# A whole new order of an attention and softplus-MLP kernel: warm-up tile moved, two batches read by split products, fillers ahead of the scores

## The chip, the cores and the metric

One core of one Trainium2 chip. The metric is the device time of one execution in microseconds, lower is better; 0.3% of it is 2.0 us. Engines: TensorE (PE; its weight loads PEld), VectorE (DVE), ScalarE (ACT), GpSimd (POOL), and SyncE (SP), which here issues every DMA.

## The reference, cut to what matters

```python
# x: (8, 8, 512, 64) = B, H, S, D;  state: (8, 8, 32, 64)
scale = 1.0 / np.sqrt(D)
a  = softmax(scale * x @ state.T)      # (B, H, 512, 32)
xread = a @ state                      # (B, H, 512, 64)
a2 = softmax(scale * state @ x.T)      # (B, H, 32, 512)
sread = a2 @ x                         # (B, H, 32, 64)
rows = concat([xread, sread], axis=2)  # heads side by side: (8 * 544, 512)
h = rows @ w_in                        # 512 -> 2048
out = softplus(h) @ w_out              # 2048 -> 512
```

(softmax subtracts the row's maximum and adds 1e-9 to the sum; softplus is max(h, 0) + log1p(exp(-|h|)). The weights come in as float64.)

## The kernel before, in words

**Work.** A batch's scores `sc` (step Q) serve both softmaxes. The one over the 32 states is done on a tile transposed in blocks: A (transpose), M (maximum), Ms (subtract it), m (exp), N (sum and reciprocal), Nm (multiply), D (transpose back), then the split ah, al. The one over the 512 rows: E (row maximum), e (exp with the sum), r (reciprocal). The states are multiplied into w_in (the V tiles), so that the MLP's hidden layer of a batch's 512 x-rows is one product per block of 128 of the 2048 hidden columns: step `h.b.f`, six matmuls of 512 columns. It is followed by softplus (`s`), its split (`gh`, `gl`) and the second layer `m.b.f.c`, three matmuls each for four row blocks c. The 256 sread rows of all batches go through the MLP together as group 8 (`h.8.u.i`, `m.8.u.i`).

**Splits.** Most products run in TensorE's fast float32r format. An operand is split into a high part (a cast on ScalarE, line 289) and a low part (a subtraction on VectorE, line 305), and three products, high by high, high by low, low by high, are added. The scores Q of batches 0 and 1 and the products V0, V1 of w_in with the states are plain f32 matmuls, which the profile shows as two records each.

**Weights.** w_in and w_out arrive as 64-bit words: `Li`, `Lo` load them, `ch`, `cu`, `cr` convert them (cr joins both halves), `wh`, `wl` split w_out, `Sw` stores converted w_in, `V0`, `V1` multiply w_in by the states, `va`, `ve` copy the products out of PSUM, `vh`, `vl` split them.

**Read of the sread rows.** `Lx` loads x; G transposes the exponentials on TensorE (four 128-column transposes), R multiplies them by x, X scales by 1/sum, T transposes to `sreadT`, which h.8 needs. For batches 2 to 7 the operands of R are split (`ph`, `pl` for the exponentials, `yh`, `yl` for x; R is eight float32r matmuls; `xc`, `xa` add two halves). For batches 0 and 1 (`WHOLE = 2`) `ga` copies the exponentials and R is four plain f32 matmuls.

**Order.** Nothing is reordered at run time. `PLAN` is one list of 2638 steps, `name:engine:places`, in the order in which they are issued; each engine takes its own in that order. Engine letters: T TensorE, V and W VectorE (W another form of `cu` with two instructions), A and C ScalarE (C a form of `ch` by a plain copy), G GpSimd, S SyncE. The number is the slot of SBUF or bank of PSUM; a step that takes a slot waits until every earlier user of that slot is done. Here the list begins

```
Lz.0:S:0 Lt.0.1.0:S:1 Lt.0.1.1:S:2 zn.0:G:3 Li.0.1:S:4 Li.0.0:S:5 Lq.1:S:6 Lq.0:S:7 Li.0.6:S:8 ...
```

and ahead of it the kernel puts the warm-up tile `idle` into slot 0, sets it to zero (line 766) and runs eight f32 matmuls on it (line 768). `Lz.0` then takes slot 0 too. TensorE's first steps are Q.0.1, V1.0.0, V0.0.0, V1.0.1, V0.0.6, Q.0.0, ...; ahead of its first h (`h.0.0`) stand four Q, thirteen V, G.0.1, G.0.0 and R.0.1.

The matmul helper is line 308, DMA loads and stores are lines 296 and 299, copies 289 (ScalarE) and 293 (VectorE), cu 337, 340 and 341, cr 345, A 453, Ms 456, Nm 466.

Of the kernel before, what the change touches and what calls it, by code (L numbers as in the profile page):

```python
# [8 lines left out]
F32 = mybir.dt.float32  # L9
# [28 lines left out]
ch.0.3:A:31 Lo.0:S:2 V0.0.1:T:6 E.0.0:V: va.0.1.1:A: va.0.1.0:A: cu.0.3:V:32 e.0.0:A:33 cr.0.2:V: cr.0.3:V: V0.0.2:T:7 ch.0.7:C:34 A.0.0:V:35
V0.0.3:T:1 e.0.1:A:36 va.0.2.0:V: M.0.0:V: va.0.3.0:A: ch.0.4:A:37 cu.0.4:V:38 vh.0.0:A:39 Lt.1.1.1:S:40 Ms.0.0:V: G.0.1:T:2 va.0.6.1:A: Lx.0.1:S:3
V1.0.6:T:3 va.0.2.1:A: cr.0.4:V: Sw.0.3:S: ch.0.5:A:41 vl.0.0:V:42 V0.0.4:T:6 m.0.0:A: Lt.1.0.1:S:43 ve.0.6:V:44 Lo.1:S:4 va.0.4.0:A: cu.0.5:V:45  # L40
zc.1.0:A: cu.0.7:W:46 Sv.0.6:S: G.0.0:T:5 zc.1.1:A: ga.0.1:A:47 cr.0.5:V: Lo.2:S:5 cr.0.7:V: ch.o0:A:48 Sw.0.4:S: V0.0.5:T:0 cu.o0:V:49 Lo.3:S:6
# [36 lines left out]
Sp.1.2.6:S: vl.0.4:V:6 Lo.14:S:13 P.1.3.7:T:4 Rl.3.1:V: F.1.5.3:S: h.0.8:T:0 Sp.0.3.0:S: vh.1.4:A:40 F.1.5.0:S: Lx.2.1:S:11 wl.9:V:38 pe.1.3.7:A:29
m.0.6.2:T: Sw.3.0:S: s.0.8:A:41 Sp.1.3.7:S: h.0.9:T:4 vl.0.5:V:2 wl.11:V:25 pe.1.2.3:V:18 h.0.11:T:0 ch.3.2:A:4 vl.1.4:V:30 Sp.1.2.3:S: gh.0.8:A:6
# [163 lines left out]
class Op:  # L243
# [594 lines left out]
```

## Time and profile before

| | |
|---|---|
| runs | 678.28, 676.57, 676.0; median 676.57 us |
| profiled execution | 675.82 us, span 674.0 us |
| TensorE busy | 660.8 us (98% of the span), 3028 matmul records |
| VectorE, ScalarE busy | 408.1 and 420.9 us |
| GpSimd busy | 1.6 us |
| DMA | 85.54 MB |

The span runs from the first to the last instruction of the profiled execution; the time has a little more around it. A row of a group gives busy time, the mean of one instruction in ns, and the idle time of the engine just before, with what ended it. Matmuls overlap, so the distance from start to start is what one costs in a stream, not its duration.

### The profile page before, as it was taken

Reading aid. Unit: us, or ns where it says so; the run is one execution under the profiler, and the core shown is the slowest. Engines: PE = TensorE matmul, PEld = TensorE weight load, DVE = VectorE, ACT = ScalarE, POOL = GpSimd, SP = SyncE. Lnnn points to the kernel's source line nnn. Section 1 sums busy time; section 2 is a strip of 40 time slices with the busy share of each in tenths; the row PEclk is TensorE's granted clock in tenths of the full one; section 3 lists DMA queues with packets and bytes.
Section 4 is the critical chain, followed back from the end, with each engine's and each line's share of the span. In section 5 each row is a group of like instructions: output and inputs, shape, how many; then the busy total and the mean of one; then the engine's idle time right before and its main releaser. Section 6 shows DMA issues by size and latency. Waiting matters only on the chain.

```text
span 674.0 us, 8950 instructions
## 1 busy us (share of the span) xinstructions
PE 660.8 (98%) x3028; PEld 540.2 (80%) x3028; DVE 408.1 (61%) x790; ACT 420.9 (62%) x746; POOL 1.6 (0%) x8
## 2 busy tenths in 40 slices
PE   6899999999999999999999999999999999999997
PEld 3576778888888888888888888888888888988886
DVE  3899969786987597452855367445846586122210
ACT  2989986767767787753765367535865658224322
POOL 0000000000000000000000000000000000000000
PEclk9999999999999999999999999999999999999999
DMA  5994368857138324621233122412076202103001
GB/s 206 376 396 154 116 232 275 312 195 236 55 112 248 89 90 134 200 65 51 92 108 88 32 94 79 118 32 94 17 245 177 71 17 79 48 1 78 1 0 63
DMA packets 54094, 85.54 MB, mean 127 GB/s; under 512 B 7456, under 2 KB 28960, under 8 KB 54048
## 3 DMA queue, kind: packets, MB, share of 16 engines
q1 hardware_dynamic: 54048, 84.96, 38.7%
q8 instruction: 24, 0.39, 0.2%
q14 instruction: 22, 0.18, 0.1%
HBM read 57.15 MB, written 27.79 MB: 126 GB/s over the span
## 4 chain that ended last, share of the span: by engine, by line
PE 91%; DVE 4%; DMA 2%; ACT 2%; issue 1%; SPq 0%; ACTq 0%
PE acc L308 53%; PE h L308 28%; PE pp L308 3%; PE rp L308 3%; PE qp L308 2%; PE gp L494 1%; DMA vd<-ve 1%; DMA w<-in_w_in_dram 1%; PE vp L308 1%; DVE wf L345 1%; PE h_idle L768 1%; DVE gL L305 1%; PE sc L308 1%; ACT Vk L289 0%; DVE Vl L305 0%
## 5 line engine op out<-in xcount | busy, mean ns | idle before, releaser
L308 PE MATMUL acc<-Wh,gH 128*128 128x512 f32 x544 | 215.3, 396 | 0.0
L308 PE MATMUL acc<-Wh,gL 128*128 128x512 f32 x544 | 212.1, 390 | 0.1
L308 PE MATMUL acc<-Wl,gH 128*128 128x512 f32 x544 | 212.1, 390 | 0.0
L305 DVE TENSOR_TENSOR gL<-t,gH 128x512 fp32r<-128x512 f32 x136 | 92.3, 686 | 172.5 <-ACT gH L289 172.2
L637 ACT ACTIVATE t<-h 128x512 f32<-128x512 f32 x136 | 79.9, 598 | 168.6 <-PE h L308 168.0
L308 PEld LDWEIGHTS acc<-Wh,gL 128*128 128x128 f32 x544 | 102.1, 188 | 22.8 <-DVE gL L305 1.2
L308 PEld LDWEIGHTS acc<-Wl,gH 128*128 128x128 f32 x544 | 102.2, 188 | 21.2 <-issue 0.9
L308 PEld LDWEIGHTS acc<-Wh,gH 128*128 128x128 f32 x544 | 102.2, 188 | 21.1 <-issue 0.7
L308 PE MATMUL h<-aH,Vh 128*128 128x512 f32 x256 | 101.9, 398 | 0.2 <-ACT Vh L289 0.2
L308 PE MATMUL h<-aH,Vl 128*128 128x512 f32 x256 | 99.9, 390 | 0.1
L308 PE MATMUL h<-aL,Vh 128*128 128x512 f32 x256 | 99.8, 390 | 0.1
L289 ACT CAST gH<-t 128x512 fp32r<-128x512 f32 x136 | 83.3, 623 | 3.5 <-PE acc L308 1.2
L308 PEld LDWEIGHTS h<-aH,Vh 128*128 128x128 f32 x256 | 48.0, 188 | 11.8 <-ACT t L637 0.8
L308 PEld LDWEIGHTS h<-aL,Vh 128*128 128x128 f32 x256 | 48.1, 188 | 10.8 <-DVE aL L305 0.9
L308 PEld LDWEIGHTS h<-aH,Vl 128*128 128x128 f32 x256 | 48.1, 188 | 10.6 <-DVE Vl L305 0.5
L305 DVE TENSOR_TENSOR Vl<-Vf,Vh 128x512 fp32r<-128x512 f32 x56 | 37.9, 683 | 10.4 <-ACT Vh L289 5.5
L289 ACT CAST Vh<-Vf 128x512 fp32r<-128x512 f32 x56 | 34.5, 620 | 2.2 <-DMA Vf<-vd 2.1
L289 ACT COPY o<-acc 128x512 f32<-128x512 f32 x30 | 16.9, 590 | 12.8 <-PE acc L308 12.4
L637 ACT ACT_TABLE_LOAD x18 | 23.1, 1283 | 2.8 <-issue 2.1
L308 PE MATMUL h<-sreadT,uH 128*128 128x256 f32 x128 | 23.4, 283 | 0.0
L308 PEld LDWEIGHTS h<-sreadT,uH 128*128 128x128 f32 x128 | 20.6, 191 | 0.8
L577 DVE TENSOR_TENSOR sc<-qp,qs 64x512 f32<-64x512 f32 x24 | 16.4, 683 | 8.0 <-ACT qs L575 7.5
(113 smaller groups left out, 726.9 us busy)
## 6 DMA issues: line engine op xcount, KB each, us to landing
vd<-px SPq DMA_DIRECT2D x48, 256.0 KB, 3.8
Vf<-vd SPq DMA_DIRECT2D x192, 64.0 KB, 2.0
xT<-in_xt_dram SPq DMA_DIRECT2D x32, 256.0 KB, 4.7
o<-in_w_out_dram SPq DMA_DIRECT2D x16, 512.0 KB, 6.7
x<-in_xn_dram SPq DMA_DIRECT2D x16, 512.0 KB, 4.7
out_dram<-o SPq DMA_DIRECT2D x32, 256.0 KB, 2.1
w<-in_w_in_dram SPq DMA_DIRECT2D x12, 512.0 KB, 6.5
Wf<-wsc SPq DMA_DIRECT2D x32, 128.0 KB, 2.8
```

The costliest lines, as they stand in the source:

```text
L289: nc.scalar.copy(dst, src)
L305: lambda e: eng(e).tensor_tensor(r(dlo()), src(), dhi(), ALU.subtract))
L308: nc.tensor.matmul(dst, lhs, rhs, start=start, stop=stop)
L345: nc.vector.scalar_tensor_tensor(u, page(f"h2.{key}", n).bitcast(I32), 3, u, ALU.logical_shift_left, ALU.bitwise_or)
L494: nc.tensor.transpose(at(f"gp.{b}.{g}")[:, P * c:P * c + P], at(src)[:, P * c:P * c + P], at("ident"))
L577: lambda e, kj=kj, sc=sc, j=j: nc.vector.tensor_tensor(at(sc)[64 * j:64 * j + 64], at(f"qp.{kj}")[0:64], at(f"qs.{kj}")[0:64], ALU.add))
L637: lambda e: nc.scalar.activation(at(f"t.{k}"), at(f"h.{k}"), AF.Softplus))
L768: nc.tensor.matmul(at("h.idle")[:, 0:P], at("idle")[:, 0:P], at("idle")[:, 0:P], start=True, stop=True)
```

## The change

- `PLAN` is written anew: order, engines and places of all steps (2636 steps). TensorE's last 382 steps are in the old order.
- The warm-up tile gets a place of its own; the first load is into a fresh slot.
- xT of a batch is one load of 1 MB in a slot of four pages (kind `q`) instead of four loads of 256 KB; batch 0's is the first load of all.
- Batches 0 and 1 read as the others do: the code of batches 2 to 7 moves into `readrows` and serves all; `ga` and the f32 R go, and T turns two 64-column blocks instead of four of 128.
- 13 elementwise steps of the head go to GpSimd: Ms and Nm of batches 0 and 1, vh.0.0, al.0.1, ah.1.0, ah.1.1, al.1.0.
- Fillers `w.i`, two transposes of the identity, may stand in the plan; six do, all ahead of the first h.
- The partial outputs of batches 0 and 1 lie in one tile `po` each instead of four.
- Six `pe` copies more run on ScalarE instead of VectorE, and two more `cu` in the W form.

TensorE's first steps now: Q.0.0, V1.0.1, Q.0.1, V0.0.3, five fillers, V1.0.0, V0.0.1, V1.0.3, V1.0.7, a filler, V0.0.7, V0.0.0, V0.0.2, V1.0.2, Q.1.1, Q.1.0, V0.0.4, V0.0.5, V0.0.6, h.0.1, h.0.0, ... The G and R steps of batch 0 come later.

```diff
+WARMERS = 60
 PLAN = """
-Lz.0:S:0 Lt.0.1.0:S:1 Lt.0.1.1:S:2 zn.0:G:3 Li.0.1:S:4 Li.0.0:S:5 Lq.1:S:6 Lq.0:S:7 Li.0.6:S:8 Lt.0.0.0:S:9 zc.0.0:V: zc.0.1:V: Lt.0.0.1:S:10
...
+Lt.0:S:0 Lz.0:S:1 zn.0:G:0 Li.0.1:S:2 Lq.1:S:3 Li.0.3:S:4 Lq.0:S:5 Li.0.0:S:6 Li.0.7:S:7 Lo.0:S:0 Lo.1:S:1 Li.0.2:S:8 zc.0.0:V: zc.0.1:V: Q.0.0:T:0
+ch.0.1:C:9 cu.0.1:W:10 cr.0.1:V: Sw.0.1:S: ch.0.3:A:11 cu.0.3:V:12 V1.0.1:T:1 E.0.0:V: Q.0.1:T:2 ve.0.1:A:13 cr.0.3:V: Sv.0.1:S: A.0.0:V:14 zn.1:G:15
+ch.0.0:A:16 Lz.1:S:17 Lt.1:S:1 cu.0.0:V:18 ch.0.7:A:19 M.0.0:V: V0.0.3:T:3 Sw.0.3:S: w.25:T:4 A.0.1:V:20 Li.0.6:S:21 va.0.3.1:A:2 Ms.0.0:G: w.26:T:5
+va.0.3.0:A:3 Li.0.5:S:22 w.27:T:6 E.0.1:V: Li.0.4:S:23 w.28:T:7 m.0.0:A: M.0.1:V: e.0.1:A:24 cr.0.0:V: N.0.0:V: Ms.0.1:G: w.32:T:1 Sw.0.0:S: V1.0.0:T:4
+ch.0.2:C:25 V0.0.1:T:5 ve.0.0:A:26 cu.0.2:W:27 V1.0.3:T:3 m.0.1:A: cu.0.7:V:28 cr.0.2:V: va.0.1.1:A: cr.0.7:V: ve.0.3:A:29 N.0.1:V: zc.1.0:A: Nm.0.0:G:
...
+SLOT = {1: "s", 2: "d", 4: "q"}
 def width(buf):
...
+    if kind in ("xT", "po"):
+        return 4
...
-            for j in range(2):
-                load(f"Lt.{k}.{j}", [f"xT.{k}.{j}"], lambda k=k, j=j: at(f"xT.{k}.{j}"), lambda b=b, g=g, j=j: io.xt[b, :, 2 * g + j, :])
...
-            op(f"ga.{k}", "AV", [f"gp.{k}"], [f"aa.{k}"], lambda e, k=k: copy(e, at(f"aa.{k}"), at(f"gp.{k}")))
-
-            def read(e, k=k):
-                for c in range(4):
-                    mm(at(f"rp.{k}")[:, 0:256], at(f"aa.{k}")[:, P * c:P * c + P], page(f"x.{k}", 4, 4 * D)[:, c], c == 0, c == 3)
...
+    for b in range(B):
+        whole = b < WHOLE
         load(f"Lz.{b}", [f"zf.{b}"], lambda b=b: page(f"zf.{b}", 4, 64), lambda b=b: io.zp[b])
+        load(f"Lt.{b}", [f"xT.{b}"], lambda b=b: page(f"xT.{b}", 4, S), lambda b=b: io.xt[b])
...
+            rowexp(b, g, sc, tok if whole else tok + [f"T.{k}:1"], ex, f"{ex}:e")
+            readrows(b, g, ex, [f"{ex}:e"])
...
+    for i in range(WARMERS):
+        def turn(e, i=i):
+            for c in range(2):
+                nc.tensor.transpose(at(f"wp.{i}")[:, P * c:P * c + P], at("ident"), at("ident"))
+
+        op(f"w.{i}", "T", [], [f"wp.{i}"], turn)
...
+    idle = cp.tile([P, P], F32, name="idle")
...
-        put("idle", 0)
         put("h.idle", 0)
-        nc.vector.memset(at("idle")[:, 0:P], 0.0)
+        nc.vector.memset(idle, 0.0)
         for _ in range(WARM):
-            nc.tensor.matmul(at("h.idle")[:, 0:P], at("idle")[:, 0:P], at("idle")[:, 0:P], start=True, stop=True)
+            nc.tensor.matmul(at("h.idle")[:, 0:P], idle, idle, start=True, stop=True)
```

`readrows(b, g, src, tok)` holds the steps G, ph, pl, yh, yl, R, xc, xa and X of lines 582 to 614 unchanged.

More of the change, by code (lines that the diff above doesn't have):

```diff
@@ L38 @@
[L38 to L41, printed above, removed]
@@ L240 @@
+o.7.0.1:A:59 m.7.15.3:T: So.7.1:S: o.7.0.2:A:58 So.7.2:S: o.7.0.3:A:12 So.7.3:S:
 """
@@ L258, in width @@
     whole = at and at[0] in map(str, range(WHOLE))
-    if kind in ("vp", "pp", "qp", "gp", "rp", "tp", "h", "acc") or kind == "sc" and whole:
+    if kind in ("vp", "pp", "qp", "gp", "rp", "tp", "h", "acc", "wp") or kind == "sc" and whole:
         return 0
-    if kind in ("o8", "x", "xs", "Wf", "Vk"):
+    if kind in ("xT", "po"):
+        return 4
+    if kind in ("o8", "x", "xs", "Wf", "Vk", "aa"):
         return 2
-    return 2 if kind == "w8" and at[0] != "0" or kind == "aa" and not whole else 1
+    return 2 if kind == "w8" and at[0] != "0" else 1
 def rounded(buf):
     kind, *at = buf.split(".")
-    return kind in ("KH", "KL", "R", "Vh", "Vl", "aH", "aL", "xh", "xl", "xs", "Wh", "Wl", "gH", "gL", "uH", "uL") \
-        or kind in ("z", "aa") and int(at[0]) >= WHOLE
+    return kind in ("KH", "KL", "R", "Vh", "Vl", "aH", "aL", "xh", "xl", "xs", "Wh", "Wl", "gH", "gL", "uH", "uL", "aa") \
+        or kind == "z" and int(at[0]) >= WHOLE
 def graph(io, at, nc):
@@ L496, in turned, with readrows, read, gather @@
         op(f"G.{b}.{g}", "T", tok, [f"gp.{b}.{g}"], f)
[L498 to L503 removed]
+    def readrows(b, g, src, tok):
+        k = f"{b}.{g}"
+        turned(b, g, src, tok)
+        pair = lambda: page(f"aa.{k}", 4, 2, 2, 64)
+        split(f"ph.{k}", f"pl.{k}", lambda: at(f"gp.{k}").rearrange("p (c j n) -> p c j n", c=4, j=2),
+              lambda: pair()[:, :, :, 0], lambda: pair()[:, :, :, 1], [f"gp.{k}"], f"aa.{k}:h", f"aa.{k}:l", "A")
+        for j in range(2):
+            kj = f"{k}.{j}"
+            xs = lambda kj=kj: page(f"xs.{kj}", 4, 2, 2 * D)
+            split(f"yh.{kj}", f"yl.{kj}", lambda j=j: page(f"x.{k}", 4, 4 * D)[:, :, P * j:P * j + P],
+                  lambda xs=xs: xs()[:, :, 0], lambda xs=xs: xs()[:, :, 1], [f"x.{k}"], f"xs.{kj}:h", f"xs.{kj}:l")
+        def read(e):
+            for j in range(2):
+                for c in range(4):
+                    mm(at(f"rp.{k}")[:, 256 * j:256 * j + 256], r(page(f"aa.{k}", 4, 2, P)[:, c, j]),
+                       r(page(f"xs.{k}.{j}", 4, 256)[:, c]), c == 0, c == 3)
+        op(f"R.{k}", "T", [f"aa.{k}:h", f"aa.{k}:l"] + [f"xs.{k}.{j}:{x}" for j in range(2) for x in "hl"], [f"rp.{k}"], read)
+        op(f"xc.{k}", "A", [f"rp.{k}"], [f"xq.{k}:1"], lambda e: nc.scalar.copy(at(f"xq.{k}")[0:64], at(f"rp.{k}")[64:128]))
+        op(f"xa.{k}", "V", [f"rp.{k}", f"xq.{k}:1"], [f"xq.{k}:2"],
+           lambda e: nc.vector.tensor_tensor(at(f"xq.{k}")[0:64], at(f"rp.{k}")[0:64], at(f"xq.{k}")[0:64], ALU.add))
+        def gather(e):
+            sv = at(f"xq.{k}")[0:64].rearrange("p (j i n) -> p j i n", j=2, i=2)
+            sr = page(f"sr.{b}", 2, 2, D)
+            rj = at(f"rj.{k}")
+            for j in range(2):
+                nc.vector.tensor_copy(rj[0:64, j:j + 1], at(f"rs.{k}")[64 * j:64 * j + 64])
+            for o in range(2):
+                rows, cs = slice(32 * o, 32 * o + 32), slice(64 * o, 64 * o + 64)
+                nc.vector.tensor_tensor(sr[rows, g], sv[rows, :, 0, cs], sv[rows, :, 1, cs], ALU.add)
+            nc.vector.tensor_tensor(sr[0:64, g], sr[0:64, g], rj[0:64].unsqueeze(2).broadcast_to([64, 2, D]), ALU.mult)
+        op(f"X.{k}", "V", [f"xq.{k}:2", f"rs.{k}:2"], [f"sr.{b}:{g}", f"rj.{k}"], gather)
@@ new lines, in graph @@
+    for b in range(B):
+        whole = b < WHOLE
+        load(f"Lz.{b}", [f"zf.{b}"], lambda b=b: page(f"zf.{b}", 4, 64), lambda b=b: io.zp[b])
+        load(f"Lt.{b}", [f"xT.{b}"], lambda b=b: page(f"xT.{b}", 4, S), lambda b=b: io.xt[b])
+        if whole:
+            op(f"zn.{b}", "G", [], [f"z.{b}:0"], lambda e, b=b: nc.gpsimd.memset(at(f"z.{b}"), 0.0))
+            for j in range(2):
+                op(f"zc.{b}.{j}", "AV", [f"zf.{b}", f"z.{b}:0"], [f"z.{b}:{j}c"],
+                   lambda e, b=b, j=j: copy(e, page(f"z.{b}", 4, P)[:, j::2, 64 * j:64 * j + 64], page(f"zf.{b}", 4, 64)[:, j::2]))
+        else:
+            z4 = lambda b=b: page(f"z.{b}", 4, 2, 64)
+            split(f"zh.{b}", f"zl.{b}", lambda b=b: page(f"zf.{b}", 4, 64), lambda z4=z4: z4()[:, :, 0], lambda z4=z4: z4()[:, :, 1],
+                  [f"zf.{b}"], f"z.{b}:h", f"z.{b}:l")
@@ L504, in graph @@
         for g in range(2):
             k = f"{b}.{g}"
-            for j in range(2):
-                load(f"Lt.{k}.{j}", [f"xT.{k}.{j}"], lambda k=k, j=j: at(f"xT.{k}.{j}"), lambda b=b, g=g, j=j: io.xt[b, :, 2 * g + j, :])
-            load(f"Lx.{k}", [f"x.{k}"], lambda k=k: page(f"x.{k}", 4, 4 * D), lambda b=b, g=g: io.xn[b, g])
-            def scores(e, b=b, g=g, k=k):
-                for j in range(2):
-                    mm(at(f"sc.{k}"), page(f"z.{b}", 4, P)[:, 2 * g + j], at(f"xT.{k}.{j}"), j == 0, j == 1)
@@ L554, in graph @@
-    for b in range(WHOLE, B):
-        load(f"Lz.{b}", [f"zf.{b}"], lambda b=b: page(f"zf.{b}", 4, 64), lambda b=b: io.zp[b])
-        z4 = lambda b=b: page(f"z.{b}", 4, 2, 64)
-        split(f"zh.{b}", f"zl.{b}", lambda b=b: page(f"zf.{b}", 4, 64), lambda z4=z4: z4()[:, :, 0], lambda z4=z4: z4()[:, :, 1],
-              [f"zf.{b}"], f"z.{b}:h", f"z.{b}:l")
-        for g in range(2):
-            k = f"{b}.{g}"
-            for j in range(2):
-                load(f"Lt.{k}.{j}", [f"xT.{k}.{j}"], lambda k=k, j=j: at(f"xT.{k}.{j}"), lambda b=b, g=g, j=j: io.xt[b, :, 2 * g + j, :])
@@ L563, in graph, with scores @@
             load(f"Lx.{k}", [f"x.{k}"], lambda k=k: page(f"x.{k}", 4, 4 * D), lambda b=b, g=g: io.xn[b, g])
             sc = f"sc.{k}"
-            for j in range(2):
+            if whole:
+                def scores(e, b=b, g=g, k=k):
+                    for j in range(2):
+                        mm(at(f"sc.{k}"), page(f"z.{b}", 4, P)[:, 2 * g + j], page(f"xT.{b}", 4, S)[:, 2 * g + j], j == 0, j == 1)
+                op(f"Q.{k}", "T", [f"z.{b}:0c", f"z.{b}:1c", f"xT.{b}"], [sc], scores)
+                tok, ex = [sc], f"e2.{k}"
@@ L566, in graph @@
+            for j in range(0 if whole else 2):
                 kj = f"{k}.{j}"
-                split(f"sh.{kj}", f"sl.{kj}", lambda kj=kj: at(f"xT.{kj}"),
-                      lambda kj=kj: at(f"xh.{kj}"), lambda kj=kj: at(f"xl.{kj}"), [f"xT.{kj}"], f"xh.{kj}", f"xl.{kj}")
+                split(f"sh.{kj}", f"sl.{kj}", lambda b=b, g=g, j=j: page(f"xT.{b}", 4, S)[:, 2 * g + j],
+                      lambda kj=kj: at(f"xh.{kj}"), lambda kj=kj: at(f"xl.{kj}"), [f"xT.{b}"], f"xh.{kj}", f"xl.{kj}")
@@ L668, in graph @@
                 acc = f"acc.{b}.{x}.{c}"
-                o, done = f"o.{b}.{c}", f"o.{b}.{c}:{x}"
+                kept = len(runs[b]) > 1
+                done = f"po.{b}:{c}.{x}" if kept else f"o.{b}.{c}"
+                o = (lambda b=b, c=c: page(f"po.{b}", 4, DM)[:, c]) if kept else (lambda b=b, c=c: at(f"o.{b}.{c}"))
                 if x == 0:
-                    op(f"o.{b}.{x}.{c}", "AV", [f"{acc}:{f1 - 1}"], [done], lambda e, o=o, acc=acc: copy(e, at(o), at(acc)))
+                    op(f"o.{b}.{x}.{c}", "AV", [f"{acc}:{f1 - 1}"], [done], lambda e, o=o, acc=acc: copy(e, o(), at(acc)))
                 else:
-                    op(f"o.{b}.{x}.{c}", "V", [f"{acc}:{f1 - 1}", f"{o}:{x - 1}"], [done],
-                       lambda e, o=o, acc=acc: nc.vector.tensor_tensor(at(o), at(acc), at(o), ALU.add))
+                    op(f"o.{b}.{x}.{c}", "V", [f"{acc}:{f1 - 1}", f"po.{b}:{c}.{x - 1}"], [done],
+                       lambda e, o=o, acc=acc: nc.vector.tensor_tensor(o(), at(acc), o(), ALU.add))
                 if x == len(runs[b]) - 1:
-                    store(f"So.{b}.{c}", [done], lambda b=b, c=c: io.out[b * ROWS + P * c:b * ROWS + P * c + P], lambda o=o: at(o))
+                    store(f"So.{b}.{c}", [done], lambda b=b, c=c: io.out[b * ROWS + P * c:b * ROWS + P * c + P], o)
     for u in range(NFT // 2):
@@ L778, in attention_then_softplus_mlp @@
             step.emit(e)
-        assert not ops
+        assert all(name.startswith("w.") for name in ops)
 _OUTS = [((B * ROWS, DM), 'float32')]
```

468 lines of the change are left out of this document (201 added, 267 removed).

## The prediction, on record before the change was timed

> **What bounds the kernel now.** I read the profile in this order: the windows table for where each engine is full, the waits of SyncE's queue, the timeline of the head, then the groups by form for prices.
>
> ```profile
> core 0: us, PE busy (x) PEld busy (x) DVE busy (x) ACT busy (x) POOL busy (x), PEclk, DMA share, GB/s
> 0.00:31.18 31.18, 22.22 (x75) 13.45 (x75) 18.09 (x48) 17.64 (x43) 1.63 (x8) 1.00 0.79 281
> 31.18:100.00 68.82, 68.32 (x282) 50.94 (x281) 61.33 (x123) 61.62 (x111) 0.00 (x0) 1.00 0.65 232
> 100.00:674.00 574.00, 570.25 (x2676) 475.81 (x2674) 328.68 (x620) 341.70 (x595) 0.00 (x0) 1.00 0.34 106
> ```
>
> The cut at 31.18 is the start of the first h matmul. Behind it TensorE is busy for 68.32 of 68.82 us and 570.25 of 574.00; the 3.7 missing at the end are the output copies and stores. So the end is the start of the first h, plus the TensorE work left behind it, plus 3.7. Only two things move the time by much: when the first h starts, and how much TensorE work stands behind it.
>
> What holds the first h back is the head:
>
> ```profile
> SPq L296 <- PE h_idle L768: 3.8, 1, 3.8
> ```
>
> ```profile
> 0.73 0.20 POOL masks.py:197 MEMSET ident<- 128x128 f32 x1 [0.29 <-POOLq L819]
> ...
> 1.05 3.78 PE L768 MATMUL h_idle<-idle 128*128 128x128 f32 x16 [1.05 <-DVE idle L766]
> ...
> 4.87 0.38 SPq L296 DMA_DIRECT2D zf<-in_zp_dram  x1
> 5.30 0.90 SPq L296 DMA_DIRECT2D xT<-in_xt_dram  x2
> ...
> 7.13 0.36 DVE L293 COPY z<-zf 128x128 f32<-128x128 f32 x2 [6.13 <-DMA zf<-in_zp_dram]
> ...
> 8.94 3.94 PE L308 MATMUL sc<-xT,z 128*128 128x512 f32 x4 [4.11 <-DMA xT<-in_xt_dram]
> ...
> 12.03 0.50 DVE L337 TENSOR_SCALAR wf<-w 128x256 int32<-128x256 int32 x2 [4.54 <-DMA w<-in_w_in_dram]
> ...
> 12.92 0.72 DVE L453 STREAM_TRANSPOSE T<-sc 128x512 f32<-128x512 f32 x1
> ...
> 15.99 1.88 PE L308 MATMUL sc<-xT,z 128*128 128x512 f32 x4
> ```
>
> The first load goes out at 4.87, although other engines begin at 0.73: SyncE stands 3.8 us behind the warm-up matmuls, because the first load's tile lies on the warm-up tile. Then the scores wait 4.11 us for xT, and VectorE has almost nothing until 12.03. From there to 31.18 VectorE is the supply:
>
> ```profile
> 5.87:8.94 3.07, 0.00 (x0) 0.03 (x1) 0.36 (x2) 0.00 (x0) 0.00 (x0) 1.00 0.62 205
> 8.94:12.03 3.09, 3.09 (x4) 0.97 (x4) 0.00 (x1) 0.44 (x2) 0.00 (x0) 1.00 0.95 329
> 12.03:31.18 19.15, 15.35 (x57) 8.96 (x55) 17.56 (x45) 15.92 (x41) 0.00 (x0) 1.00 1.03 371
> 31.18:80.00 48.82, 48.35 (x196) 35.98 (x195) 47.21 (x96) 44.70 (x79) 0.00 (x0) 1.00 0.69 251
> ```
>
> 45 VectorE instructions fill 17.56 of 19.15 us there, one per 0.426 us with its small waits. Behind it, to 80, VectorE is still busy 47.21 of 48.82.
>
> **The change, part by part.** *TensorE work removed.* The reads of batches 0 and 1 lose their two-record f32 products:
>
> ```profile
> L308 PE MATMUL rp<-xs,aa 128*128 128x256 f32 x96 | 12.8, 283 | 0.0
> ...
> L308 PE MATMUL rp<-x,aa 128*128 128x256 f32 x32 | 7.7, 382 | 0.0
> L494 PE MATMUL gp<-ident,sc 128*128 128x128 f32 x48 | 6.5, 272 | 0.0
> ...
> L618 PE MATMUL tp<-ident,sr 64*128 64x64 f32 x12 | 2.0, 247 | 0.0
> L540 PE MATMUL tp<-ident,sr 128*128 128x128 f32 x8 | 1.2, 271 | 0.0
> ```
>
> ```profile
> 28.30 1.74 PE rp L308 x8
> ...
> 362.54 1.91 PE rp L308 x16
> ```
>
> By the chain, one old read is 1.74 us (8 records) and one split read 0.955 (half of 1.91): four reads save 3.1. The turns go from 8 records (1.2) to 4 of the other kind (2.0 x 4/12 = 0.7): 0.5. Together 3.6 us of TensorE time, which nothing hides behind the first h.
>
> *Work moved past the first h.* Before, two G steps and R.0.1 run ahead of it; now none. A G step is four transposes of 6.5/48: 0.54; two are 1.1. Thirteen V products and four Q stand ahead of it in both orders. So behind the first h stand four split reads (3.8) where three old ones stood (5.2), cheaper turns (-0.5) and two more G (+1.1): **-0.8 us**; the rest of the 3.6 is saved ahead of it. The six fillers in the new order (12 transposes, 1.6 us by the same row) all lie ahead of the first h, where TensorE had 3.8 us free between 12.03 and 31.18; without that cover they cost at most 1.6.
>
> *Start of the loads.* With the warm-up tile in its own place SyncE can issue at about 0.75, 4.1 us earlier. But the first scores now need Lt.0 whole (1.05 MB) and then Lz.0 (0.13 MB), against 0.66 MB that were there 4.07 us after the first issue (4.87 to 8.94). The further 0.52 MB cost 1.6 us at 329 GB/s and 2.5 at 205; I take 1.9, nearer the later row, as one long transfer has no gaps between issues. First scores: 0.75 + 4.07 + 1.9 = 6.7, and 2.2 us of the 4.1 remain.
>
> *First scores.* Before they ran at half rate (3.94 us for 4 records, 1.88 later). The warm-up ends at about 4.83 as before, and 1.9 us of idling follow instead of 4.11. I take the half rate again, by its nearest row: Q.0.0 ends at 6.7 + 3.94 = 10.6. At the later rate it would end at 8.6; that is the low end. The Trainium skill, "TensorE: Matmul & The Clock Gate", section "Part 1: The HAM clock gate", says that about 3.4 us of sustained work release the clock and about as long an idle window takes it back; by it these scores could run at full rate after a gap of 1.9, some 2 us better. The trace agrees as far as that sixteen records in 3.78 us and a gap of 4.11 left them slow; it shows no gap of 1.9.
>
> *VectorE up to the first h (now h.0.1).* In the new order 34 VectorE instructions stand from E.0.0 to cr.0.5, on which TensorE's V0.0.5 depends, and V0.0.6 with h.0.1 behind it. At 0.426 each that is 14.5: 10.6 + 14.5 = 25.1, then V0.0.5 and V0.0.6, 0.4 each: **first h at 26.0**, 5.2 earlier. Ms, Nm and al.0.1 of this chain are on GpSimd, and their cover is VectorE's other work.
>
> *GpSimd's price.* The trace has no elementwise step of GpSimd. Its nearest rows:
>
> ```profile
> L500 POOL MEMSET z<- 128x512 f32 x2 | 1.0, 524 | 0.0
> masks.py:199 POOL TENSOR_SCALAR_AFFINE_SELECT ident<-ident 128x128 f32<-128x128 f32 x1 | 0.3, 292 | 0.1
> ```
>
> Low end 0.52 (a pass that only writes); high end 2.3, twice the select's 0.29 scaled by four. I take 1.1, the select scaled once, as it too reads and writes. The chain of six (Ms twice, Nm twice, vh.0.0, al.0.1) starts when M.0.0 ends, six VectorE instructions (2.6) after E.0.0 begins, at 13.2: 6 x 1.1 = 6.6 inside the 12.8 us to 26.0. At 2.3 it is 13.8 and would put the first h at 27.0, 1.0 later. A page of the Trainium skill, "GPSIMD Engine Reference", section "3.1 Elementwise — side-by-side cycle accounting", gives 4497 ns for an f32 tensor_tensor of 2048 columns; by it a step of 512 is an estimated 1.1 and the sum stays.
>
> *VectorE and ScalarE behind the first h.*
>
> ```profile
> L305 DVE TENSOR_TENSOR xs<-x,xs 128x512 fp32r<-128x512 f32 x24 | 15.4, 685 | 1.5 <-ACT xs L289 1.3
> ...
> L456 DVE TENSOR_TENSOR T<-T,mx 128x512 f32<-128x512 f32 x16 | 10.6, 683 | 0.1
> ...
> L601 DVE TENSOR_TENSOR xq<-rp,xq 64x512 f32<-64x512 f32 x12 | 8.0, 680 | 5.1 <-ACT xq L599 5.1
> L305 DVE TENSOR_TENSOR aa<-gp,aa 128x512 fp32r<-128x512 f32 x12 | 7.9, 686 | 11.5 <-ACT aa L289 11.5
> ```
>
> The split reads add 8 yl (5.5), 4 pl (2.7) and 4 xa (2.7): 10.9 us on VectorE, and casts of like number on ScalarE. Eight Ms and Nm and two al leave for GpSimd: 10 x 0.68 = 6.8. The net, 4.1, falls into a stage that had 1.6 us free (48.82 less 47.21) and now begins earlier. Cover: the order puts these reads where TensorE has h and acc work, and their result is needed only by h.8, far later. Low end 0, high end 4.1 if TensorE has to wait for all of it; I take **+1.0**, nearer 0, since TensorE lost only 0.5 us in 68.82 with VectorE as full as that.
>
> *At nothing:* the output's partial sums in one po tile (no instruction more or less), 24 fewer SyncE issues behind the head (TensorE covers them), the tail (same steps and engines). A whole xT load waits for every reader of its slot; SyncE issues it a batch ahead of its use. Without that cover each costs the 0.79 MB that it brings beyond a quarter, 2.4 us at 329 GB/s.
>
> **Sum.** First h -5.2, work behind it -0.8, fuller VectorE +1.0: -5.0. The profiled execution took 675.82 (span 674.0), which gives 670.8; the median of the runs, 676.57, lies 0.75 above it, which gives 671.6. I take 671.0 between them.
>
> **The rivals.** *Warm and early.* The first scores run at full rate and the long load at the later row's speed: first h at 23.7, another 2.3 off, and no squeeze, 1.0 off: 667.7. For it: the gap of 1.9 is half the old one. Against: the warm-up itself never left the slow rate. Chance 0.19.
>
> *The head gains nothing.* VectorE's order, not the loads, keeps the first h near 31: GpSimd's steps at the high end, the long load in front, each link late by a little. Then only the -0.8 of work and the squeeze remain: 675.82 - 0.8 + 1.0 = 676.0. For it: VectorE was 92% full from 12.03 on, and an earlier load doesn't make it faster. Against: those 4.54 us of waiting ahead of 12.03. Chance 0.14.
>
> *GpSimd holds VectorE up (slower).* If a VectorE instruction with two SBUF inputs stands still while a GpSimd step reads SBUF, each of the 13 steps can hold VectorE by up to its own 1.1: 14.3 us, in a stage where VectorE has 1.6 free. It eats the gain from (5.0 + 1.6)/13, that is 0.5 us a step, and is slower by over 0.3% from 0.7. At the full price it is 671.0 + 14.3 - 1.6 = **683.7**. For it: the xs subtractions above and the joins of the weights read two SBUF tiles. Against: of the 34 instructions ahead of h.0.1 only 9 (seven joins, al, vl) do. The Trainium skill, "SBUF — State Buffer", section "Who interferes with whom", states such a lock between these two kinds of instruction, held for a whole instruction; no row of this trace can show it. Chance 0.11, of which 0.07 over 678.6.
>
> **Chances.** Main case (668.5 to 674.0) 0.56, warm and early 0.19, no gain in the head 0.14, GpSimd's hold 0.11. 0.3% of 676.57 is 2.0 us, about what a measurement here can tell from no change: faster than 674.5 are the first two, 0.02 of the third and 0.03 of the fourth, 0.80; the same 0.13; slower 0.07. Range 664.5 to 676.5: it takes in the warm case with room, the upper bounds of the GpSimd price (+1.0) and of the squeeze (+3.1), and half of the third case, and leaves out about 0.04 below and 0.15 above. The main case's own is 668.5 to 674.0.
>
> **What would show it.** SyncE's first load at 0.7 to 0.9, with no wait for h_idle; scores at about 6.7, slow; first h at 26; no f32 rp records and 12.8 + 4.3 us of split ones; GpSimd steps of about 1.1. Wrong if the first h starts behind 29, if GpSimd's steps take over 2.3 us or VectorE's subtractions beside them grow beyond 0.68, or if TensorE's busy share between first h and 100 falls by more than 2 us.

## The result, and the profile after

The new order takes 672.58 us (median, 672.02 to 673.18) against 676.62 for the kernel before in the same measurement: 0.9939 of it, with an interval of 0.9923 to 0.9955. The forecast was 671.0, range 664.5 to 676.5, faster. The gain is 4.0 us where the sum said 5.0.

The profiled execution took 673.18, the highest of its four, with a span of 671.4. Its windows, cut at the first h as before (the columns are length, busy time of each engine with its instructions, clock, DMA share, GB/s):

```profile
core 0: us, PE busy (x) PEld busy (x) DVE busy (x) ACT busy (x) POOL busy (x), PEclk, DMA share, GB/s
0.00:27.74 27.74, 21.25 (x70) 13.69 (x71) 17.96 (x43) 15.09 (x37) 8.15 (x14) 1.00 0.91 325
27.74:100.00 72.26, 70.31 (x306) 53.37 (x304) 70.62 (x134) 68.04 (x121) 8.39 (x7) 1.00 0.74 248
100.00:671.40 571.40, 567.64 (x2665) 473.09 (x2663) 328.44 (x627) 341.88 (x595) 0.00 (x0) 1.00 0.32 103
```

The first h starts at 27.74, 3.4 earlier than 31.18. From there to 100 TensorE is idle for 1.95 us (before: 0.50), and VectorE is busy for 70.62 of 72.26 (before: 61.33 of 68.82): it is nearly full now. By the windows, the span splits at the first h into

| profile | first h | from first h to the end | TensorE busy in it | TensorE idle in it (3.7 of it the tail) | span |
|---|---|---|---|---|---|
| before | 31.18 | 642.82 | 638.57 | 4.25 | 674.0 |
| after | 27.74 | 643.66 | 637.95 | 5.71 | 671.4 |
| difference | -3.4 | +0.8 | -0.6 | +1.5 | -2.6 |

Busy time is not quite work: the same instructions are busy for 639.07 us in the old kernel with its warm-up tile moved (below). So busy and idle are known to about half a microsecond, their sum better. The difference of the spans is less than that of the medians, as the profiled execution was the longest of its kernel, and the one before the shortest. A second profile of the same kernel (below, the last experiment) has its first h at 26.87, 643.63 from there to the end, and a span of 670.5. The head of the new kernel, from the timeline (start, duration, and in brackets the idle time before it with its releaser):

```profile
0.74 0.39 SPq L300 DMA_DIRECT2D xT<-in_xt_dram  x1
...
1.05 3.78 PE L744 MATMUL h_idle<-idle 128*128 128x128 f32 x16 [1.05 <-DVE idle L742]
1.19 0.42 SPq L300 DMA_DIRECT2D zf<-in_zp_dram  x1
...
5.99 0.36 DVE L297 COPY z<-zf 128x128 f32<-128x128 f32 x2 [4.99 <-DMA zf<-in_zp_dram]
...
6.31 3.75 PE L312 MATMUL sc<-xT,z 128*128 128x512 f32 x4 [1.48 <-DVE z L297]
...
9.60 0.29 DVE L341 TENSOR_SCALAR wf<-w 128x256 int32<-128x256 int32 x1 [0.30 <-DMA w<-in_w_in_dram]
...
10.10 0.69 DVE L479 TENSOR_REDUCE nm<-sc 128x1 f32<-128x512 f32 x1 [0.21 <-PE sc L312]
...
10.71 2.75 PE L312 MATMUL sc<-xT,z 128*128 128x512 f32 x4
...
27.74 0.58 PE L312 MATMUL h<-aH,Vh 128*128 128x512 f32 x1
```

The loads go out at 0.74, beside the warm-up and not behind it. The scores come at 6.31, and slow: 3.75 us for four records. The clock column of that stretch reads 1.00 only because the trace has no clock record before 12.46; from there it records the full clock (more in the last section). E.0.0, the line at 10.10, is the 34-instruction chain's first link. Half of the second four scores, those ahead of 12.46, are slow as well (2.75 where 1.88 is usual).

GpSimd's new steps, from the groups by form (busy us, mean ns of one), and the reads:

```profile
L470 POOL TENSOR_TENSOR T<-T,sm 128x512 f32<-128x512 f32 x4 | 4.8, 1197 | 13.5 <-DVE sm L466 11.4 <-ACT ve L293 2.1
L460 POOL TENSOR_TENSOR T<-T,mx 128x512 f32<-128x512 f32 x4 | 4.7, 1189 | 15.6 <-DVE mx L458 15.6
L309 POOL TENSOR_TENSOR aL<-af,aH 128x512 fp32r<-128x512 f32 x2 | 2.9, 1435 | 1.0 <-ACT aH L293 0.9
L295 POOL TENSOR_SCALAR aH<-af 128x512 fp32r<-128x512 f32 x2 | 2.0, 978 | 0.3 <-PE acc L312 0.3
...
L295 POOL TENSOR_SCALAR Vh<-Vk 128x512 fp32r<-128x512 f32 x1 | 0.6, 618 | 0.9 <-ACT Vk L293 0.9
```

```profile
L312 PE MATMUL rp<-xs,aa 128*128 128x256 f32 x128 | 17.2, 282 | 0.0
...
L584 PE MATMUL tp<-ident,sr 64*128 64x64 f32 x16 | 2.8, 250 | 0.0
```

Thirteen steps take 15.0 us together, 1.15 each. What the groups don't show stands in the timeline, VectorE's instructions beside GpSimd's:

```profile
17.28 1.09 POOL L470 TENSOR_TENSOR T<-T,sm 128x512 f32<-128x512 f32 x1 [0.47 <-DVE sm L466]
17.39 1.14 DVE L341 TENSOR_SCALAR wf<-w 128x256 int32<-128x256 int32 x1
...
23.43 0.28 DVE L341 TENSOR_SCALAR wf<-w 128x256 int32<-128x256 int32 x1
...
23.90 1.55 POOL L309 TENSOR_TENSOR aL<-af,aH 128x512 fp32r<-128x512 f32 x1 [0.93 <-ACT aH L293]
24.24 1.50 DVE L349 SCALAR_TENSOR_TENSOR wf<-h,wf 128x256 int32<-128x256 int32 x1
...
30.30 1.43 DVE L309 TENSOR_TENSOR Vl<-Vk,Vh 128x512 fp32r<-128x512 f32 x1
...
40.69 1.54 DVE L309 TENSOR_TENSOR gL<-t,gH 128x512 fp32r<-128x512 f32 x1
...
47.08 1.31 POOL L309 TENSOR_TENSOR aL<-af,aH 128x512 fp32r<-128x512 f32 x1
47.20 2.35 DVE L349 SCALAR_TENSOR_TENSOR wf<-h,wf 128x512 int32<-128x512 int32 x2
...
49.09 0.67 PE L312 MATMUL vp<-wf,QZ 128*128 128x512 f32 x1 [1.33 <-DVE wf L349]
```

The same TENSOR_SCALAR takes 0.28 alone and 1.14 beside a GpSimd step; it ends 0.16 after that step (18.53 and 18.37). The join at 24.24 takes 1.50 where its form takes 0.41, and the subtractions at 30.30 and 40.69 take 1.43 and 1.54 where theirs takes 0.68. At 47.20 TensorE waits 1.33 us for such a join. Ten VectorE instructions are longer than their form by 0.1 to 1.1 us each, 5.8 us in all, every one beside a GpSimd step: 0.44 us per step. Four of them lie ahead of the first h: 0.14 + 0.86 + 0.24 + 1.09 = 2.3 us.

### The profile page after: what moved, and what is told of

Read it like the earlier page. It is cut to its first block, busy times and chain, and to the rows that moved or that the text cites. A ratio compares the mean times of both kernels' runs of the same rounds, so it can differ in the third digit from the quotient of the medians.

```text
span 671.4 us, 8968 instructions
## 1 busy us (share of the span) xinstructions
PE 659.2 (98%) x3036; PEld 540.2 (80%) x3036; DVE 417.0 (62%) x802; ACT 425.0 (63%) x751; POOL 16.5 (2%) x21
## 4 chain that ended last, share of the span: by engine, by line
PE 90%; ACT 5%; DVE 2%; DMA 2%; issue 1%; SPq 0%; DVEq 0%; ACTq 0%
PE acc L312 52%; PE h L312 28%; PE pp L312 3%; PE rp L312 2%; PE qp L312 2%; PE sc L312 1%; ACT Vk L293 1%; PE gp L498 1%; DMA x<-in_xn_dram 1%; PE vp L312 1%; DVE wf L349 1%; DMA zf<-in_zp_dram 1%; ACT t L611 1%; ACT gH L293 0%; ACT L611 0%
## 5 line engine op out<-in xcount | busy, mean ns | idle before, releaser
L312 PEld LDWEIGHTS acc<-Wl,gH 128*128 128x128 f32 x544 | 102.2, 188 | 21.1 <-DVE Wl L309 0.7
L293 ACT COPY o<-acc 128x512 f32<-128x512 f32 x26 | 14.6, 587 | 13.3 <-PE acc L312 12.7
L312 PE MATMUL vp<-wf,QZ 128*128 128x256 f32 (+1 forms) x48 | 17.1, 469 | 5.3 <-DVE wf L349 5.3
L309 DVE TENSOR_TENSOR xs<-x,xs 128x512 fp32r<-128x512 f32 x32 | 20.4, 685 | 1.9 <-ACT xs L293 1.9
```

Source lines behind the costliest of these rows:

```text
L293: nc.scalar.copy(dst, src)
L309: lambda e: eng(e).tensor_tensor(r(dlo()), src(), dhi(), ALU.subtract))
L312: nc.tensor.matmul(dst, lhs, rhs, start=start, stop=stop)
```

## The experiments

**The warm-up tile's place alone.** First put back in the new order, then moved alone in the old one.

```diff
 # in the kernel after
-    idle = cp.tile([P, P], F32, name="idle")
...
+        idle = sp.tile([P, 512 * 4], F32, tag="q0", name="idle", bufs=1)[:, 0:P]
```

> The changed kernel with the warm-up tile back in the slot of the first load (here the slot of xT of batch 0). Theory: SyncE waits for the warm-up matmuls again, first load at 4.9, first h 3.5 to 4.1 later (31.2 to 31.9), time 676.1 to 676.7: no gain is left of the whole change. Rival: the new order has room in the head, first h by 30, time 674 or less.

676.54 us, 1.0006 [0.9997, 1.0015] of before: nothing is left of the gain. SyncE's wait is back, and the scores come 4.1 us later than in the kernel after:

```profile
SPq L300 <- PE h_idle L744: 3.8, 1, 3.8
```

```profile
10.41 3.75 PE L312 MATMUL sc<-xT,z 128*128 128x512 f32 x4 [5.58 <-DVE z L297]
```

```diff
 # in the kernel before
+    idle = cp.tile([P, P], F32, name="idle")
...
-        put("idle", 0)
...
-        nc.vector.memset(at("idle")[:, 0:P], 0.0)
+        nc.vector.memset(idle, 0.0)
...
```

> The kernel before (676.6), with nothing changed but a place of its own for the warm-up tile. Theory (the start of the loads decides): first load at about 0.75 instead of 4.87, the old head moves as a whole, first h at 27 to 28 instead of 31.2, time 672.5 to 673.5, that is most of the whole gain. Rival (VectorE's order decides and not the loads): VectorE starts earlier but the first h comes at 30 or later, time 675.5 to 676.6.

671.32 us, 0.9924 [0.9911, 0.9938]: one tile gives 4.95 us, all that the whole change gives; the time lies below the theory's 672.5 to 673.5. With the small first loads of the old order the scores start at 5.26, a microsecond ahead of the new order's:

```profile
0.74 0.38 SPq L296 DMA_DIRECT2D zf<-in_zp_dram  x1
...
5.26 2.29 PE L308 MATMUL sc<-xT,z 128*128 128x512 f32 x4 [0.43 <-DMA xT<-in_xt_dram]
```

First h at 27.00, and 643.40 from there to the end. Against this kernel the rest of the change gains nothing that shows: its first h is about where this one has it (26.87 and 27.74 in two profiles), and from there to the end it takes 643.63 and 643.66.

**GpSimd does none of the 13 steps.** Ms, Nm and al go to VectorE, the casts to ScalarE.

```diff
-... Ms.0.0:G: ... Ms.0.1:G: ... Nm.0.0:G: ... vh.0.0:G:37 ... al.0.1:G:50 ...
+... Ms.0.0:V: ... Ms.0.1:V: ... Nm.0.0:V: ... vh.0.0:A:37 ... al.0.1:V:50 ...
```

> The changed kernel (672.6) with its 13 GpSimd steps given back: Ms, Nm and al to VectorE, vh.0.0 and both ah to ScalarE. Theory (VectorE stands still beside GpSimd's reads): the ten long VectorE instructions of the changed kernel, 5.8 us over their forms' usual time, fall back to the usual time, among them the 1.50 us weight join just ahead of the first h (usual 0.41). Against that ten steps of 0.68 come back, 6.8 us. So the two cancel to about 1 us: first h 27.2 to 29, time 672.0 to 674.0. Rival (GpSimd's relief is where the gain comes from, the long instructions are chance or DMA): the long instructions stay and 6.8 us come on top, first h beyond 30, time 676 or more.

671.78 us, 0.9933 [0.9920, 0.9945], 0.8 below the median after (0.4 by the ratios to before), and just below the theory's 672.0 to 674.0; the rival's 676 is out. No VectorE instruction is longer than its form, and the join ahead of the first h is short:

```profile
24.52 0.43 DVE L349 SCALAR_TENSOR_TENSOR wf<-h,wf 128x256 int32<-128x256 int32 x1 [0.40 <-ACT h L332]
```

VectorE does ten more steps (6.8 us by 0.68 each) and the kernel is no slower for it. First h 26.95, and 643.05 from there to the end, 0.6 less than after. The steps given to GpSimd bought nothing net.

**Only the two al on VectorE.** These are the steps beside which TensorE's joins were held.

```diff
-... al.0.1:G:50 ... al.1.0:G:44 ...
+... al.0.1:V:50 ... al.1.0:V:44 ...
```

> The changed kernel with al.0.1 and al.1.0 alone given back to VectorE; the other 11 GpSimd steps stay. These two (1.55 and 1.31 us) lie beside the two longest weight joins, 1.50 ahead of the first h and 1.75 ahead of TensorE's 1.5 us gap at 47. Theory (it matters where a GpSimd step lies): both joins fall to their usual 0.41 and 0.68, first h at 26.6 to 27.2, the gap at 47 falls to 0.5 or less, time 670.8 to 671.8. Rival (VectorE needs all the relief it can get): the two steps of 0.68 cost what the joins gain, 672.2 to 673.

671.51 us (669.59 to 671.9), 0.9924 [0.9912, 0.9936]. The excess on VectorE falls from 5.8 to 3.7 us, TensorE's wait for the join at 47 falls from 1.33 to 0.26, and from the first h to the end it takes 643.25, 0.4 less than after. The first h, at 24.55, can't be put down to the edit alone: the profiled execution is the fastest of the five, with fast first scores (1.95 us behind a gap of 1.52) and weights that reached VectorE at 8.67.

**A longer warm-up.** 12 loops of it, 24 records, instead of 8.

```diff
-WARM = 8
+WARM = 12
```

> The changed kernel with 12 warm-up matmuls instead of 8, so that TensorE works until about 6.2, where the first scores start (6.31). Theory A (sustained work lifts the rate): the first scores take 1.9 us and not 3.75, Q.0.1 ends about 1.5 earlier; but E.0.0 stands on VectorE behind the second weight conversion, which waits for its load until 9.6, so that only 0.5 to 1.0 us reach the first h: time 671.6 to 672.2. Theory B (the rate doesn't follow): scores still at 3.75, time 672.4 to 672.8. Theory C (the scores decide alone): 2 us, 670.6.

671.33 us, 0.9927 [0.9914, 0.9939], a little below theory A's 671.6 to 672.2.

```profile
6.41 1.96 PE L312 MATMUL sc<-xT,z 128*128 128x512 f32 x4 [0.32 <-PE h_idle L744]
...
9.59 0.29 DVE L341 TENSOR_SCALAR wf<-w 128x256 int32<-128x256 int32 x1 [0.26 <-DMA w<-in_w_in_dram]
...
9.80 0.68 DVE L479 TENSOR_REDUCE nm<-sc 128x1 f32<-128x512 f32 x1
...
26.54 0.58 PE L312 MATMUL h<-aH,Vh 128*128 128x512 f32 x1
```

The scores are fast and done at 8.4, but E.0.0 starts only 0.3 us earlier than after: it stands behind the instruction at 9.59, whose weights have just landed. The rest of the 1.2 us at the first h comes from the second four scores, which are fast too.

**The first xT in two loads, behind z.**

```diff
-Lt.0:S:0 Lz.0:S:1 zn.0:G:0 ...
+Lz.0:S:1 Lt.0.0:S:0 Lt.0.1:S: zn.0:G:0 ...
...
```

> The changed kernel with batch 0's xT in two loads again, zf ahead of them, so that Q.0.0 needs 0.66 MB as in the old order. Theory: first scores at 5.2 to 5.4 instead of 6.31, and at the full rate, as after a gap of 0.43 us in the old order with the warm-up tile moved (first scores 5.26, four records done by 7.54). But E.0.0 stays behind the second weight conversion, whose load lands at 9.6, so about 1.2 us are won, as with the longer warm-up: first h 26.3 to 26.8, time 671.0 to 671.7. Rival (the scores decide alone): the whole 2.5 us, first h about 25.2, time 670.0.

671.91 us, 0.9938 [0.9926, 0.9950], no more than 0.7 below the kernel after, within what the runs of one kernel differ by, and 0.2 above the theory's range. Scores at 5.54 instead of 6.31, but still slow (3.75) behind a gap of 0.71, where the theory had the full rate; first h 26.45, as it said.

**The reads of batches 0 and 1 done twice.** The split products of these two batches are computed a second time over the first, each pass starting its sums anew, so the result stays the same.

```diff
-            for j in range(2):
+            for j in [0, 1] * (2 if b < WHOLE else 1):
```

> The changed kernel with the split read R of batches 0 and 1 computed twice over (the second overwrites the first), 32 matmul records more, 3.8 us of TensorE by the chain. Theory (TensorE is full behind the first h): the time grows by 3.4 to 3.9, to 676.0 to 676.5. Rival (the early reads fill TensorE's gaps): by less than 1.5, to 674.0 or less; then the split reads saved nothing either.

```profile
L312 PE MATMUL rp<-xs,aa 128*128 128x256 f32 x160 | 21.1, 282 | 0.0
```

675.37 us, 0.9987 [0.9979, 0.9995]: 2.8 us above the median after (3.2 by the ratios). The records take 3.9 us more (21.1 for 17.2), and the time from the first h to the end grows by 2.9 (646.59 for 643.66), so about a microsecond goes into TensorE's waits. The time lies 0.6 below the theory's range and 1.4 above the rival's: a microsecond of TensorE work there does cost most of a microsecond of time.

**No fillers.** The six w steps are left out of the order.

> The changed kernel without the six fillers. Theory (they lie in TensorE's waits and are worth nothing, as TensorE works often enough without them): 672.2 to 672.9, first h within 0.3 of 27.74. Rival A (they keep the rate up): the V products behind Q.0.1 run slow without them, first h 1 us or more later, 673.6 or more. Rival B (they stand in the way): up to 1.3 us earlier, 671.3.

672.28 us, 0.9944 [0.9931, 0.9957]: no effect that can be told. The first h, at 26.71, is near the 26.87 of the second profile of the kernel after. In this profile the scores were fast (1.96) behind a gap of 1.81, with the same 16 warm-up records.

**Combinations, with the kernel after once more beside them.** The three edits above are put together as named.

> Two edits of earlier runs at once: al.0.1 and al.1.0 on VectorE (two of GpSimd's longest steps gone) and 12 warm-up matmuls instead of 8. Theory A (the two losses are separate and both lie ahead of the first h or in the join gap at 47 us): the gains of the two single edits add, 1.1 + 1.2 = 2.3 us under the new order: 670.3; scores done by 8.4, first h at about 24.6. Theory B (what is won ahead of the first h is given back behind it, as VectorE sets the pace there): no better than either alone, 671.3 to 671.5, and the gaps behind the first h grow by about 1.

669.73 us (669.53 to 670.49), 0.9912 [0.9898, 0.9926]: 3.1 us below the kernel after in the same measurement, where the two single gains were 1.1 and 1.2. They add, to a little below the 670.3 of theory A, and this version beats the kernels before and after. Against the old kernel with its tile moved (0.9911 to 0.9938) the intervals overlap, and there the longer warm-up was not tried.

```profile
8.65 0.29 DVE L341 TENSOR_SCALAR wf<-w 128x256 int32<-128x256 int32 x1 [0.73 <-DMA w<-in_w_in_dram]
8.86 0.68 DVE L479 TENSOR_REDUCE nm<-sc 128x1 f32<-128x512 f32 x1
...
22.10 0.41 DVE L349 SCALAR_TENSOR_TENSOR wf<-h,wf 128x256 int32<-128x256 int32 x1
...
24.52 0.58 PE L312 MATMUL h<-aH,Vh 128*128 128x512 f32 x1
```

Here the weights landed 0.9 earlier than in the run with the longer warm-up alone, and the fast scores count in full; the join at 22.10 is free of the hold, 1.1 us. That makes the 2.0 us between the two first h's, and from there to the end it takes 643.28 for 643.66. The profile is like that of the two al steps alone (first h 24.55), where the scores were fast by chance.

> GpSimd does none of the 13 steps, and 12 warm-up matmuls. Theory A (GpSimd's hold and the slow scores are separate): 671.8 - 1.0 = 670.7, scores done by 8.4, first h at about 25.5. Theory B (VectorE's ten more steps, 6.8 us, set the pace whatever the head does): 671.5 to 671.8.

671.72 us, 0.9935 [0.9922, 0.9948], no better than without the longer warm-up (671.78). The scores were fast, yet the first h came at 27.91, and the windows say why:

```profile
13.35:16.76 3.41, 1.38 (x6) 1.06 (x6) 3.31 (x9) 2.10 (x5) 0.00 (x0) 1.00 1.06 376
16.76:20.17 3.41, 2.04 (x7) 1.52 (x7) 3.34 (x12) 3.17 (x9) 0.00 (x0) 0.50 1.03 383
20.17:23.58 3.41, 3.41 (x9) 2.68 (x8) 2.25 (x5) 2.15 (x6) 0.00 (x0) 0.50 0.71 248
```

```profile
19.72 3.62 PE L312 MATMUL vp<-wf,QZ 128*128 128x256 f32 x8
```

TensorE got a clock of 0.50 from 16.76 to 23.58, behind a stretch in which it was busy for 1.38 of 3.41 us; eight V records took 3.62 us where 1.89 is usual. In this profile the loss hides whatever the fast scores gave, so the run doesn't decide between the two expectations. Its fastest run, 670.80, is near the lower one; the two runs with a granted clock of 0.995, the profiled one among them, are its slowest (672.82 and 672.01).

> The edits of e9 and the first xT in two loads behind z. Theory A: scores at 5.6 and at full rate, done by 7.6, first h at about 24: 0.5 to 0.8 less than e9, 669.6 to 670. Theory B: the first h waits for the weights' load that lands at 9.6 and for VectorE behind it, so earlier scores bring nothing: as e9, 670.3.

670.49 us, 0.9921 [0.9908, 0.9934], no better than without the split load. The scores ended at 7.87 and E.0.0 started at 9.29, behind the weights that had landed at 9.1: with fast scores the bound of the head is that load.

> The new order unchanged, beside the three others on the same chip, once more for the rate of its first scores. Theory A (the rate behind a gap of 1.5 us differs from run to run): the time stays at 672.0 to 673.2, and the scores take either 3.8 or about 2 us; where they take 2, first h comes at about 26.7. Theory B (the rate is settled by the order): 3.8 us again and first h at 27.7.

672.85 us (671.91 to 673.0), 0.9949 [0.9936, 0.9962].

```profile
10.42 1.88 PE L312 MATMUL sc<-xT,z 128*128 128x512 f32 x4
...
26.87 0.58 PE L312 MATMUL h<-aH,Vh 128*128 128x512 f32 x1
```

The time and the rate fit either expectation, the first h neither: the first four scores were slow again, 3.75, and yet it came at 26.87. The 0.87 us between the two profiles of this kernel is the second four scores: 2.75 in the first, with VectorE idle for 0.79 us behind them, and 1.88 here. What slow first scores cost depends on the weights. In the first profile, where these landed at 9.6, it is 0.3 us at E.0.0. Here they reached VectorE at 8.70, and E.0.0 waited 1.12 us for the scores, until 10.12; with fast scores and the same weights it began at 8.88 (the run with the two al steps).

## Why the prediction was right or wrong, by its steps

- **Start of the loads:** 0.74, as said. This step is as large as the whole gain, shown from both sides: put back alone it takes 4 us away, made alone it gives 4.95. I had it as one part of the -5.2 in the head.
- **First scores:** 6.31 for 6.7, at half rate as taken; done at 10.06 for 10.6. That they were slow behind a gap of 1.48 was luck as much as reading: with the same warm-up they were fast behind gaps of 1.52 and 1.81 in two other profiles.
- **First h:** 27.74 (26.87 in the second profile) for 26.0. The mis-sized term is VectorE's chain from E.0.0 to cr.0.5: 14.5 by the sum, 10.10 to 26.81 = 16.7 in the profile. Of that 2.3 is GpSimd's hold and 0.8 the slow second scores. The remaining 13.6 for 34 instructions is 0.40 each, near the 0.426 that I took.
- **GpSimd's price:** 1.15 for 1.1; the rows hold. What failed is that I counted a step moved to GpSimd as off VectorE's time. The rival "GpSimd holds VectorE up" was right as a mechanism, at 0.44 us a step, and wrong in its sum, which at that price gives 671.0 + 13 x 0.44 - 1.6 = 675.1. Only 2.3 of the 5.8 us lie in the head's chain, and of the 3.4 behind the first h little reaches TensorE (without GpSimd's steps that stretch is 0.6 shorter). Against the 5.8 us stand the 6.8 that the moved steps save, so without GpSimd the kernel is as fast or a little faster. A sign of being wrong came with it: subtractions beside GpSimd's steps grew beyond 0.68, to 1.43 and 1.54. The Trainium skill, "SBUF — State Buffer", section "Who interferes with whom", has instructions with two SBUF inputs contend with a GpSimd instruction that reads SBUF, and names tensor_scalar among those that can; the joins at 24.24 and 47.20 and the TENSOR_SCALAR at 17.39 (1.14 for 0.28) agree. My argument against it, that only 9 of the 34 instructions have two inputs, left out the one-input kind, which gave 1.2 of the 2.3 us.
- **Work behind the first h:** -0.6 in busy time for -0.8; split records 17.2 us (said 17.1), turns 2.8. The sign and the groups are right, and the doubled reads show that it counts.
- **Fuller VectorE:** +1.5 in idle time for +1.0. VectorE is busy for 70.62 of 72.26. The single largest wait, 1.33 at 47, is for a held join. From the first h to the end the kernel after takes 0.8 more than the one before, and without GpSimd's steps 0.2 more: the steps on GpSimd cost 0.6 there, net of what they take off VectorE. How much of the rest is VectorE's own load one profile of each doesn't show.
- **Together:** the sum had -5.2 for the head and +0.2 behind it; the profiles have -3.4 and +0.8 (-4.3 and +0.8 in the second). The path of the main case held (earlier loads, an earlier first h, TensorE full behind it); its gain in the head was 1 to 2 us too high.
- **At nothing:** the fillers cost nothing (672.28 without them).
- **The warm rival:** fast scores were open in every run, but its 667.7 didn't come. Fast scores end ahead of the weights' load, on which the chain stands next.

## What to carry to other kernels

Look first for what the first load waits for: one tile's place was worth as much as a whole new order. A step moved to another engine is free only if the instructions that run beside it keep their durations; compare each with the same form when it stands alone. And when a wait in the head is shortened, name the next load in line, since the gain ends where that lands. One profile of a head is one draw: look at the rate of its first matmuls before an edit is credited with an earlier start.

## What the runs showed that was not expected

- The rate of the first scores. With the same 16 warm-up records in 3.8 us, the first four scores took 3.75 us behind gaps of 0.71, 1.47, 1.48, 1.50 and 1.54, and 1.95 to 1.96 behind 1.52 and 1.81. So the gap doesn't decide. With 24 records and a gap of about 0.3 or less they took 1.96 to 1.98 in all four profiles. The Trainium skill, "TensorE: Matmul & The Clock Gate", section "Part 1: The HAM clock gate", puts the release of the clock at around 4 us of sustained work, give or take 0.5 from run to run. The traces here, which record when the full clock was granted, have it 3.2 to 5.5 us behind the start of the warm-up (1.05) where the warm-up released it, and else only at 10 or later:

| profile | warm-up records | full clock from | first four scores, at | took |
|---|---|---|---|---|
| before | 16 | 12.99 | 8.94 | 3.94 |
| after | 16 | 12.46 | 6.31 | 3.75 |
| after, second profile | 16 | 10.10 | 6.33 | 3.75 |
| GpSimd does none | 16 | 10.61 | 6.30 | 3.75 |
| first xT in two loads | 16 | 10.63 | 5.54 | 3.75 |
| reads done twice | 16 | 10.04 | 6.37 | 3.75 |
| no fillers | 16 | 4.28 | 6.44 | 1.96 |
| two al on VectorE | 16 | 5.58 | 6.36 | 1.95 |
| old kernel, tile moved | 16 | 5.93 | 5.26 | 2.29 |
| longer warm-up | 24 | 5.47 | 6.41 | 1.96 |
| two al on VectorE, longer warm-up | 24 | 5.79 | 6.33 | 1.96 |
| no GpSimd, longer warm-up | 24 | 6.52 | 6.59 | 1.98 |
| the same, first xT in two loads | 24 | 4.58 | 5.91 | 1.96 |

In these thirteen profiles a record of batch 0's scores that ends ahead of that time takes 1.06 to 1.19 us, and one that starts behind it 0.59 to 0.70. The run with the tile shared again shows the clock both ways: granted at 4.86, lost at 8.27 behind 3.41 us without work, and back at 15.10, with its slow scores (10.41, 3.75) in between (columns as in the windows above):

```profile
4.86:8.27 3.41, 0.00 (x0) 0.00 (x0) 0.00 (x0) 0.00 (x0) 0.00 (x0) 1.00 0.63 204
8.27:10.41 2.14, 0.00 (x0) 0.03 (x1) 0.32 (x2) 0.00 (x0) 0.00 (x0) 0.50 0.97 357
10.41:15.10 4.69, 4.68 (x7) 2.44 (x8) 2.13 (x8) 0.91 (x3) 0.00 (x0) 0.50 1.03 375
15.10:17.00 1.90, 1.90 (x6) 0.92 (x6) 1.83 (x5) 0.99 (x3) 0.10 (x1) 1.00 1.01 402
```

The stretches between two changes of the clock are multiples of 3.413 us in all 14 profiles (3.41, 6.83, 10.24, 658.77), and these steps lie differently against the start of each execution: for one and the same kernel the change came at 12.46 and at 10.10, which is no whole step apart. In 12 of the 14 profiles TensorE was busy for 3.2 us or more of the step that ended in the first grant, in the other two for 2.67 and 2.99; steps with up to 2.75 busy passed without one. So whether a warm-up of 3.8 us releases the clock depends on how it falls on the steps, and a longer one makes it likelier. What share of a step is needed stays open, and length and gap were not varied apart.

- The clock can be lost in the head even after fast scores: 0.50 for 6.83 us, with 18.2 us from E.0.0 to the first h where the same order without it took 16.9. The step ahead of the loss had TensorE busy for 1.38 us; in other profiles steps with 1.53 kept the clock.
- The second load of w_in, issued behind the same loads on the same queue, reached VectorE between 8.65 and 10.04 us in the profiles of the new order with the warm-up tile in its own place. With fast scores the first h moves with it: between the two combinations that have al on VectorE it goes from 8.65 to 9.09, and the first h from 24.52 to 24.96. Why the landing differs the runs don't show.
